# Who issues the loads: first-head loads moved to ScalarE, and the spare products spread out again

## The chip, the cores and the metric

One core of one Trainium2 chip. The metric is the device time of one execution in microseconds (us), lower is better. A run of the kernel is timed as a whole; the profile comes from one profiled execution, whose span runs from its first to its last instruction.

## The reference

The inputs are q, k, v and f_logit of shape (4, 8, 768, 48): batch, heads, tokens, head dimension. Weights are w_ch1 (384 x 1536) and w_ch2 (1536 x 384).

```python
f = 1 / (1 + exp(-f_logit))
for t in range(768):                       # per batch and head
    state = f[t, :, None] * state + outer(k[t], v[t])
    y[t] = q[t] @ state
x = y.transpose(0, 2, 1, 3).reshape(4, 768, 384)
u = x + real(fft(fft(x, axis=1), axis=2))
un = (u - mean(u)) / sqrt(var(u) + 1e-6)   # over the 384 channels
out = u + relu(un @ w_ch1) @ w_ch2
```

## The kernel before

Two heads make a **unit**; there are sixteen units, four to a batch. One head sits on partitions 0 to 47 of a tile and the other on 64 to 111 (`ROWS[0]`, `ROWS[1]`), tokens innermost. For every unit four things are read from memory: the gate logits `f` into `g`, then `k`, `q` and `v`. The `g`, `k` and `q` tiles come in two transfers of 144 KB each, one per head (r = 1 first, then r = 0), `v` in one of 288 KB. There are three buffers for `g` and `k` and four for `q`, used in turn, so a load of unit u overwrites what unit u - 3 (or u - 4) has used.

The generator `attention` works on one unit in steps, and each `yield` ends a step. By number: (1) ScalarE turns the logits into a log-gate with Exp and Ln (L330, L331); (2) VectorE scans it along the tokens (L337) and VectorE and GpSimd copy the ends of the chunks (L338, L339); (3) ScalarE takes three exponentials (L342, L343, L345); (4) VectorE multiplies q and k by two of them (L349, L350); (5) TensorE makes the scores (L361); (6) VectorE masks them (L368); (7) TensorE transposes, and ScalarE copies the result out (kT, L508); (8) to (12) are state, outputs and their transposes on TensorE, with copies by ScalarE (yT, L553 to L557, and x, L566); (13) `fold` combines tokens on VectorE and GpSimd.

After four units of a batch are done, `fnet` (letter F) computes the Fourier part (z, mid, mix), and `projected` (letter P) the two weight products: `up` at L750 with its relu on ScalarE at L752, and the second product at L759 or L773. H steps normalise.

The order of all this is written out by hand in one string, `ORDER`. Every engine's instructions are issued in the order of its words, and each engine works through its own list in order. A number advances that unit by one step. `L3fk` loads f and k of unit 3, `r` fetches one block of weights (`raw`) through SyncE, `R` three of them, `C` converts a block (ScalarE L238, VectorE L240 and L241, GpSimd L242), `T` loads the Fourier tables (`tab`, `wave`), `G` and `I` clear tiles, `W` combines weights, and `D` is `busy`: four spare bf16 products of 128 x 256 on TensorE (L153), whose result nobody reads.

All direct loads stand on SyncE's queue (SP), in ORDER's order: L166 for v, L170 for f, k and q, L267 for raw weights, L175 to L191 for the tables. If a transfer's buffer isn't free, SP waits and everything behind it on SP waits too. ScalarE (ACT) issues only one transfer, the last store (L624). The diff touches `load` and ORDER.

Of the kernel before, what the change touches and what calls it, by code (L numbers as in the profile page):

```python
# [12 lines left out]
C = 128  # L13
# [11 lines left out]


ORDER = (
    "Gq2 r I D Gq0 L0f Gk1 L1f D Gk0 L0q i D Gq3 C Gq1 Z L0k 0 D 1 Gk2 0 L1q 1 L1k D D D D D D D D D D D "
    "D 0 0 1 0 r 1 L2f 0 2 C L1v 1 L3fk 1 3 L0v 0 1 L2q 2 0 0 r 1 L2k 3 1 0 2 r 3 L3q 2 L2v 0 C L3v C "
    "L4fk R 4 2 2 3 1 0 C 2 4 1 3 L5qv D L4qv L5fk 3 D D 3 2 0 2 3 2 3 C r 4 1 4 L6fk C r 2 5 4 L6qv 4 2 "  # L30
    "1 5 6 3 4 D 4 C 5 3 T 3 6 4 5 5 4 2 r L7fk 7 5 D L7qv 3 5 S L8fk C 4 7 6 6 5 F0 5 r r F0 F0 F0 7 4 "
    "C F0 L9fk 5 6 8 H0 H0 6 5 6 r H0 C L8qv 6 7 L9qv P0 6 7 r C P0 7 7 C 9 P0 r r 5 8 C r C F0 r 7 F0 6 "
    "P0 5 9 C 6 7 P0 r C P0 8 8 C P0 r r 7 P0 P0 8 9 H0 C P0 P0 8 7 8 C P0 H0 7 9 6 H0 H0 C 9 r C P0 9 "
    "L10fk r 9 P0 r C 9 L11fk 10 C 6 P0 11 4 P0 P0 P0 P0 P0 P0 10 P0 P0 P0 L10qv P0 P0 7 F1 9 P0 F1 H0 9 "
    "W P0 P0 P0 11 F1 P0 L11qv P0 P0 P0 9 P0 P0 P0 8 L12fk P0 11 11 8 P0 P0 10 11 F1 P0 11 11 10 L14fk "
    "F1 8 P0 14 F1 P0 10 P0 8 10 P0 P0 H1 H1 10 L12qv P0 P0 10 P0 F1 P0 11 11 10 P0 10 H1 P0 P0 P0 P0 12 "
    "12 12 P0 P0 12 P0 H1 P0 12 P0 H1 L13fk P1 P1 P1 P1 P1 14 13 P1 12 8 8 P1 P1 12 9 10 L13qv 13 P1 P1 "
    "L14qv 9 P1 12 11 P1 H1 11 10 P1 P1 13 P1 13 P1 12 P1 P1 14 P1 14 V 13 P1 c V 10 P1 P1 P1 P1 P1 V "
    "L15fk P1 13 P1 11 V P1 P1 P1 P1 c P1 11 F2 V c F2 F2 H1 13 H1 F2 c 14 P1 c V c P1 P1 12 P1 P1 14 P1 "
    "P1 13 V V V P1 15 F2 c P1 12 P1 P1 P1 P1 c P1 H2 14 15 V V P1 P1 P1 P1 P1 13 P1 14 F2 P1 c P1 P1 15 "  # L40
    "V 13 P1 H2 P1 P1 L15qv P1 14 13 P1 V 12 H2 F2 14 P2 P2 P2 P2 P2 P2 P2 15 P2 P2 P2 c c 12 H2 V H2 15 "
    "H2 15 P2 c P2 15 P2 P2 15 P2 14 13 15 P2 P2 14 P2 P2 15 13 P2 P2 P2 P2 P2 H2 V 15 P2 P2 14 15 H2 P2 "
    "P2 P2 P2 15 F3 F3 P2 F3 F3 P2 F3 c P2 P2 P2 P2 P2 V P2 c P2 V c c V P2 P2 P2 P2 P2 c P2 F3 F3 P2 V "
    "P2 H3 P2 P2 P2 H3 H3 P2 P2 P2 P2 P2 P2 P2 P2 P2 P2 P3 H3 c P3 P3 P3 P3 V P3 c P3 P3 P3 c V V c P3 "
    "P3 P3 H3 P3 P3 P3 P3 P3 P3 c P3 P3 V P3 H3 P3 P3 P3 P3 P3 P3 H3 H3 P3 P3 P3 P3 P3 P3 P3 P3 P3 P3 P3 "
    "P3 V P3 P3 P3 P3 P3 c P3 c P3 P3 P3 M P3 P3 P3 P3 P3 P3 P3 P3 P3 P3 P3 P3"
)

PAIRS = ((0, 3), (2, 5), (1, 4))
# [4 lines left out]
def kernel(  # L54
# [13 lines left out]
    nc = tc.nc  # L68
    B, HP, _, D, _, S = qkf.shape
# [8 lines left out]
    R = 64 + D  # L78
    ROWS = [slice(64 * r, 64 * r + D) for r in range(2)]
# [79 lines left out]
    def load(u, *names):  # L159
        if u >= B * HP:  # L160
            return
        b, hp = divmod(u, HP)
        for name in names:
            if name == "v":
                v_of[u] = p3.tile([128, NCH, 2 * D], F32, tag="v", name=f"v{u}")
                nc.sync.dma_start(out=v_of[u], in_=v[b, hp])  # L166
                continue
            t, i = {"f": (g_t[u % 3], 2), "k": (k_t[u % 3], 1), "q": (q_t[u % 4], 0)}[name]
            for r in (1, 0):
                nc.sync.dma_start(out=t[ROWS[r]], in_=qkf[b, hp, r, :, i])  # L170

    def tables():

# [201 lines left out]
    def attention_by_blocks(u, x_all):  # L375
# [114 lines left out]
        T = double(64, T)  # L490
        yield
        load(u + 3, "f")
        yield from outputs(u, x_all, AT, Q, K, None, T)
        load(u + 3, "k")

    def outputs(u, x_all, AT, Q, K, te, T=None):
# [61 lines left out]
        if te is None:  # L558
            load(u + 4, "q", "v")
# [415 lines left out]
```

## Time and profile before

| | us |
|---|---|
| median of 3 runs (range) | 554.13 (553.52 to 554.17) |
| the profiled execution itself | 554.13 |
| its span | 552.4 |
| TensorE matmul busy (4186 instructions) | 528.4 |
| VectorE busy | 298.6 |
| ScalarE busy | 192.6 |
| GpSimd busy | 95.5 |

So 1.7 us of the execution lie outside the span. The mean granted TensorE clock is 0.981 of full speed. The page gives busy time by engine, busy shares in 40 equal slices of 13.8 us each, the DMA queues, the chain of work that ended last and the costliest groups. A group's busy time says how much work there is, not whether anybody waited for it; that is what the chain of waits and the timeline are for. Rows marked SPq or ACTq are transfers being issued by that engine's sequencer.

### The profile page before, as it was taken

What the parts mean: (1) busy time and instruction counts of PE and PEld (TensorE: products, weight loads), DVE (VectorE), ACT (ScalarE), POOL (GpSimd) and SP (SyncE); (2) the same over time, 40 slices, a digit from 0 to 9 for tenths busy, and PEclk for the clock granted to TensorE, in tenths of its full rate; (3) what the DMA queues carried; (4) which work ended last, traced back from release to release, by engine and by line L of the source; (5) the groups of instructions that cost most, each with busy time, mean ns of one, the idle gap of its engine ahead of it and who ended that gap; (6) DMA issues with size and microseconds to landing.
All of it is one profiled execution on the core that took longest, in us unless ns stands there. A gap on an engine that the chain in (4) does not pass through costs nothing.

```text
span 552.4 us, 10204 instructions
## 1 busy us (share of the span) xinstructions
PE 528.4 (96%) x4186; PEld 463.3 (84%) x4186; DVE 298.6 (54%) x534; ACT 192.6 (35%) x497; POOL 95.5 (17%) x147
## 2 busy tenths in 40 slices
PE   6888699999999999999999999999999999999995
PEld 5776578876898889889889899899889798989985
DVE  8999899984936427425644344444452442413231
ACT  5766476671332432541340422321411303021110
POOL 7156635434001000120101001003001000010000
PEclk9797799999999999999999999999999999999999
DMA  8989645363202100412530401002002004000001
GB/s 226 258 223 228 196 122 160 123 185 97 64 0 72 43 2 2 116 44 82 162 115 15 115 1 58 30 1 87 1 28 87 1 11 161 0 30 0 30 2 34
DMA packets 18398, 44.38 MB, mean 80 GB/s; under 512 B 3109, under 2 KB 4710, under 8 KB 18342
## 3 DMA queue, kind: packets, MB, share of 16 engines
q1 hardware_dynamic: 17094, 39.89, 25.8%
q0 software_dynamic: 1104, 3.54, 1.8%
q8 instruction: 35, 0.57, 0.4%
q10 hardware_dynamic: 144, 0.20, 0.1%
q14 instruction: 21, 0.17, 0.1%
HBM read 38.90 MB, written 4.72 MB: 79 GB/s over the span
## 4 chain that ended last, share of the span: by engine, by line
PE 87%; DMA 4%; DVE 3%; ACT 2%; SPq 1%; POOL 1%; issue 1%; ACTq 0%; POOLq 0%
PE up L750 34%; PE fx L773 16%; PE fz L773 12%; PE z L650 4%; PE y L537 3%; PE y L544 3%; PE po L759 3%; PE mix L669 3%; PE sc L361 3%; PE ds L517 2%; DMA g<-in_qkf_dram 2%; PE yt L564 2%; PE pt L708 1%; DMA raw<-in_w_ch_dram 1%; PE st L506 1%; DMA tab<-in_seq_tab_dram 1%
## 5 line engine op out<-in xcount | busy, mean ns | idle before, releaser
L750 PE MATMUL up<-unT,w 128*128 128x256 f32 x864 | 197.0, 382 | 1.5 <-DVE x L728 0.9
L750 PEld LDWEIGHTS up<-unT,w 128*128 128x128 f32 x864 | 161.0, 190 | 26.1 <-issue 1.5
L752 ACT ACTIVATE h<-up 128x256 f32<-128x256 f32 x144 | 55.2, 383 | 199.4 <-PE up L750 199.4
L617 POOL DMA_INDIRECT out_dram<-x,place x16 | 16.9, 1059 | 268.9 <-DVE x L803 232.0
L773 PE MATMUL fx<-block,h 128*128 128x192 f32 x264 | 46.5, 326 | 0.0
L773 PE MATMUL fx<-w,h 128*128 128x192 f32 x264 | 44.9, 327 | 0.1
L773 PEld LDWEIGHTS fx<-w,h 128*128 128x128 f32 x264 | 43.1, 190 | 0.8 <-ACT h L752 0.4
L773 PEld LDWEIGHTS fx<-block,h 128*128 128x128 f32 x264 | 43.5, 190 | 0.0
L242 POOL TENSOR_TENSOR w<-w,raw 128x384 uint32<-128x384 uint32 x24 | 30.3, 1267 | 47.6 <-ACT raw L238 19.1
L780 DVE TENSOR_TENSOR s<-h,h 128x768 f32<-128x768 f32 x11 | 10.5, 954 | 50.3 <-ACT h L752 50.3
L368 DVE COPY_PREDICATED at<-causal,sc 128x768 f32<-128x768 uint32 x32 | 31.2, 1030 | 0.8 <-PE sc L361 0.8
L337 DVE TENSOR_TENSOR_SCAN W<-g,bound 112x768 f32<-112x768 f32 x16 | 28.0, 1751 | 1.6 <-issue 0.9
L361 PE MATMUL sc<-q,W 48*64 48x128 f32 x768 | 24.9, 273 | 3.7 <-issue 1.4
L725 DVE TENSOR_TENSOR x<-mix,x 128x384 f32<-128x384 f32 x12 | 6.7, 556 | 39.0 <-PE mix L669 39.0
L361 PEld LDWEIGHTS sc<-q,W 48*64 48x64 f32 x768 | 20.9, 133 | 7.5 <-issue 3.6
L537 PE MATMUL y<-at,v 128*64 128x128 f32 (+1 forms) x384 | 26.9, 292 | 0.0
L537 PEld LDWEIGHTS y<-at,v 128*64 128x64 f32 (+1 forms) x384 | 23.2, 140 | 3.0 <-issue 3.0
L773 PE MATMUL fz<-w,s 128*128 128x192 f32 x132 | 23.5, 328 | 0.0
L773 PE MATMUL fz<-block,h 128*128 128x192 f32 x132 | 23.5, 328 | 0.0
L773 PE MATMUL fz<-w,h 128*128 128x192 f32 x132 | 23.4, 327 | 0.0
L544 PE MATMUL y<-q,stt 48*48 48x128 f32 x320 | 22.3, 285 | 0.0
L773 PEld LDWEIGHTS fz<-w,s 128*128 128x128 f32 x132 | 21.6, 190 | 0.3 <-issue 0.3
(145 smaller groups left out, 734.2 us busy)
## 6 DMA issues: line engine op xcount, KB each, us to landing
raw<-in_w_ch_dram SPq DMA_DIRECT2D x24, 384.0 KB, 4.4
g<-in_qkf_dram SPq DMA_DIRECT2D x32, 144.0 KB, 4.5
q<-in_qkf_dram SPq DMA_DIRECT2D x32, 144.0 KB, 4.0
k<-in_qkf_dram SPq DMA_DIRECT2D x32, 144.0 KB, 4.6
v<-in_v_dram SPq DMA_DIRECT2D x16, 288.0 KB, 5.2
k<-in_w_ch_dram SPq DMA_DIRECT2D x12, 384.0 KB
g<-in_w_ch_dram SPq DMA_DIRECT2D x12, 384.0 KB, 5.5
out_dram<-x SPq DMA_DIRECT2D x4, 168.0 KB
```

What stands on the lines that cost most here:

```text
L242: nc.gpsimd.tensor_tensor(bits, bits, lo, ALU.add)
L337: nc.vector.tensor_tensor_scan(W, g, bound[:R], 0.0, ALU.add, ALU.min)
L361: nc.tensor.matmul(ps[64 * s:64 * s + 64, r, i * C:(i + 1) * C], lhsT=W[ROWS[r], o + 64 * s:o + 64 * s + 64], rhs=Q[ROWS[r], o:o + C], sta ...
L368: nc.vector.copy_predicated(AT[:, :, half], causal.bitcast(U32).unsqueeze(1).unsqueeze(1).to_broadcast([128, 2, NCH // 2, C]), ps[:, :, :N ...
L537: nc.tensor.matmul(y[FILL[r], c * C:(c + 1) * C], lhsT=vt[:, c, r * D:r * D + (64 if r == 0 else D)], rhs=AT[:, r, c], start=(c % 4 == 0), ...
L544: nc.tensor.matmul(y[ROWS[r], c * C:(c + 1) * C], lhsT=st[ROWS[r], :, c - 1], rhs=Q[ROWS[r], c * C:(c + 1) * C], start=False, stop=True, s ...
L617: nc.gpsimd.indirect_dma_start(out=out.rearrange("b s d -> (b s) d"), out_offset=bass.IndirectOffsetOnAxis(ap=place[:, b, i:i + 1], axis=0 ...
L650: nc.tensor.matmul(z[:, cols], lhsT=src[:, j, lo:hi], rhs=tab[:, t, T % 2, cols], start=(i == 0), stop=(i == len(parts) - 1), skip_group_c ...
L669: nc.tensor.matmul(mix[:, o], lhsT=zz[:rows_of[T], T, PLACES[c]], rhs=cd[:rows_of[T], T, :NQ - odd], start=(i == 0), stop=(i == 1))
L750: nc.tensor.matmul(pp[:, :256], lhsT=w1[:, kt, m * 128:(m + 1) * 128], rhs=unT[:, kt], start=(kt == 0), stop=(kt == 2))
L752: nc.scalar.activation(hs[-1][:, m % H].rearrange("p t n -> p (t n)"), pp[:, :256], AF.Relu)
L773: nc.tensor.matmul(out, lhsT=h[:, m], rhs=blocks[i][:, m], start=(start and m == 0), stop=(m == H - 1), skip_group_check=True)
```

## The change

Two things. First, `load` issues the transfers of the first head (r = 0) of f, k and q through ScalarE; those of the second head (r = 1), and v, stay with SyncE. Second, the words `D` of ORDER are placed differently: the block of twelve after `L1k` shrinks to one, and thirteen are put elsewhere, mostly one by one. ORDER has 21 `D` before and 23 after. With all `D` left out, both ORDER strings are the same word by word.

```diff
-    "Gq2 r I D Gq0 L0f Gk1 L1f D Gk0 L0q i D Gq3 C Gq1 Z L0k 0 D 1 Gk2 0 L1q 1 L1k D D D D D D D D D D D "
-    "D 0 0 1 0 r 1 L2f 0 2 C L1v 1 L3fk 1 3 L0v 0 1 L2q 2 0 0 r 1 L2k 3 1 0 2 r 3 L3q 2 L2v 0 C L3v C "
-    "L4fk R 4 2 2 3 1 0 C 2 4 1 3 L5qv D L4qv L5fk 3 D D 3 2 0 2 3 2 3 C r 4 1 4 L6fk C r 2 5 4 L6qv 4 2 "
-    "1 5 6 3 4 D 4 C 5 3 T 3 6 4 5 5 4 2 r L7fk 7 5 D L7qv 3 5 S L8fk C 4 7 6 6 5 F0 5 r r F0 F0 F0 7 4 "
...
+    "Gq2 r I D Gq0 L0f Gk1 L1f D Gk0 L0q i D Gq3 C Gq1 Z L0k 0 D 1 Gk2 0 L1q 1 L1k D 0 0 1 0 r 1 L2f 0 2 "
+    "C L1v 1 L3fk D 1 3 L0v 0 1 L2q 2 0 0 r D 1 L2k 3 1 0 2 r 3 L3q 2 L2v D 0 C L3v D C L4fk R D 4 2 2 3 "
+    "1 0 C 2 4 1 3 L5qv D L4qv L5fk 3 D D 3 2 0 2 3 2 3 C r 4 1 4 L6fk C r 2 5 4 D L6qv 4 D 2 1 5 6 3 4 "
+    "D 4 C 5 3 D T 3 6 4 5 5 4 2 r L7fk 7 5 D L7qv 3 5 S L8fk C 4 7 6 6 5 F0 5 r r F0 F0 F0 7 4 C F0 "
+    "L9fk 5 6 8 H0 H0 6 5 6 r D D H0 D C L8qv 6 7 L9qv P0 6 7 r C P0 7 7 C 9 P0 r r 5 8 C r C F0 r 7 F0 "
+    "6 P0 5 9 C 6 7 P0 r C P0 8 8 C P0 r r 7 P0 P0 8 9 H0 C P0 P0 8 7 8 C P0 H0 7 D 9 6 H0 H0 C 9 r C P0 "
...
+    "9 W P0 D P0 P0 11 F1 P0 L11qv P0 P0 P0 9 P0 P0 P0 8 L12fk P0 11 11 8 P0 P0 10 11 F1 P0 11 11 10 "
...
             for r in (1, 0):
-                nc.sync.dma_start(out=t[ROWS[r]], in_=qkf[b, hp, r, :, i])
+                queue = nc.scalar if r == 0 else nc.sync
+                queue.dma_start(out=t[ROWS[r]], in_=qkf[b, hp, r, :, i])
```

## The prediction, made before the changed kernel was run

> **What bounds the kernel now.** I read the page's slices first, then busy time by stages of 10 us, the chain of waits, SP's waits and ScalarE's timeline up to 70 us.
>
> ```profile
> PE   6888699999999999999999999999999999999995
> PEclk9797799999999999999999999999999999999999
> DMA  8989645363202100412530401002002004000001
> ```
>
> TensorE is full from the sixth slice on. In the first five, 69 us, it isn't, its granted clock drops, and the DMA engines are at eight or nine tenths. So time can be won or lost in two ways: by what delays the start, and by what adds TensorE work later. The busy-time windows confirm it (columns: window and length, busy us of PE, PEld, DVE, ACT and POOL with instruction counts, PE clock, DMA share, GB/s).
>
> ```profile
> 10.00:20.00 10.00, 7.40 (x132) 6.06 (x131) 9.89 (x13) 7.92 (x13) 2.68 (x9) 0.95 1.04 249
> 20.00:30.00 10.00, 9.55 (x151) 8.68 (x151) 9.13 (x14) 7.43 (x15) 1.08 (x3) 0.71 1.04 261
> 70.00:80.00 10.00, 10.00 (x116) 8.05 (x114) 9.40 (x17) 7.18 (x24) 4.29 (x3) 0.99 0.37 100
> 90.00:100.00 10.00, 10.00 (x101) 8.45 (x100) 9.62 (x19) 6.96 (x18) 5.90 (x6) 1.00 0.46 149
> ```
>
> From 10 to 30 us the DMA engines are saturated at about 250 GB/s. From 70 us TensorE has no idle time to give back, so a delay at 70 us stays to the end. The timeline shows how closely SP runs ahead of ScalarE:
>
> ```profile
> 8.64 0.89 SPq L170 DMA_DIRECT2D g<-in_qkf_dram  x2
> 12.88 0.78 SPq L170 DMA_DIRECT2D g<-in_qkf_dram  x2
> 14.57 0.48 ACT L345 ACTIVATE te<-deep,low 112x240 f32<-112x240 f32 x1
> 14.96 0.83 ACT L330 ACTIVATE g<-g 112x768 f32<-112x768 f32 x1
> 17.21 0.83 ACT L330 ACTIVATE g<-g 112x768 f32<-112x768 f32 x1
> 20.60 0.63 ACT L508 COPY kT<-st 128x560 f32<-128x560 f32 x1 [1.60 <-PE st L506]
> 23.15 0.89 SPq L170 DMA_DIRECT2D g<-in_qkf_dram  x2
> 30.45 0.84 ACT L330 ACTIVATE g<-g 112x768 f32<-112x768 f32 x1 [0.69 <-DMA g<-in_qkf_dram]
> 57.19 0.64 ACT L566 COPY x<-yt 128x576 f32<-128x576 f32 x1 [0.89 <-PE yt L564]
> 64.48 0.84 ACT L330 ACTIVATE g<-g 112x768 f32<-112x768 f32 x1 [6.65 <-DMA g<-in_qkf_dram]
> ```
>
> SP issues f of unit 2 at 8.64, of unit 3 at 12.88, of unit 4 at 23.15. ScalarE uses them at 14.96, 17.21 and 30.45: leads of 6.3, 4.3 and 7.3 us. SP can do this because it isn't held by ScalarE's computing.
>
> [...] the DMA share is 1.04 with one issuer, and one load costs SP about 0.43 us. [...] no row of this trace shows a transfer issued by ScalarE between two ACTIVATEs[...]. [...] mean clock 0.71 from 20 to 30 us, and 24 products y take 2.82 us at 48.16 against 1.52 at 29.48.
>
> **Part one, the loads.** All 48 r = 0 transfers of f, k and q leave SP and stand in ScalarE's list where ORDER has them: 48 x 0.43 = 20.6 us of issuing. The only ACTq issue of the trace takes 0.38, so ScalarE pays 18 to 21 us of sequencer time, most beside idle ACT (192.6 busy of 552.4). The price that matters is lead. For landing I use 5.5 us: the issue table gives medians of 4.0 to 4.6, but for 0 to 35 us, under saturation, 4.7 to 5.7.
>
> *Unit 2.* ORDER has `1 L2f 0 2`: the load now stands behind unit 1's exponentials. Their last releaser (the copy of `deep` on GpSimd) is done at 12.0, so a sequencer that runs ahead issues at about 12.3 and the logits land at 17.8. Exp of unit 2 moves from 14.96 to 17.8.
>
> *Unit 3.* `2 C L1v 1 L3fk D 1 3`: the sequencer was held at Exp of unit 2 until 17.8, issues then (17.9), and the landing is at 23.4, against 17.21 now. ScalarE is in order, so kT of unit 0, behind it, starts after Exp and Ln (0.95 + 0.84) at 25.2 instead of 20.60: **+4.6**. The products ds and y of unit 0 wait for that, and with them the start.
>
> *Unit 4.* `0 C L3v D C L4fk R D 4`: the load stands behind the yT copies, which wait for y at 27.6 + 4.6 = 32.2. Issued at 32.3, landed at 37.8; without a new stall Exp would be at 30.45 + 4.6 = 35.05: **+2.8**, together +7.4.
>
> *Units 5, 6, 8 and 9* have their load two or more ScalarE groups ahead of Exp (unit 6: about 42.5 for 48.80), so I put nothing; the cover is ScalarE's copies, and if it went they would cost up to 2 us each.
>
> *Unit 7.* `L7fk 7`: again no distance. But ScalarE already stands here for 6.65 us waiting for this tile, with 10 us from issue to landing behind the tables on SP. Now r = 0 is issued at the x copy, 57.19 + 7.4 + 0.1 = 64.7, and lands at 70.2, against 64.48: **+5.7** remains of +7.4. The SP half should be no later, since SP has issued nine loads fewer by then.
>
> *After 70 us* ScalarE's relus stand behind the moved loads: 0.4 to 0.8 us each time. L10f and L11f come late for their Exp by 1 to 2 us, but ScalarE's next relu after those is only at 137.25, 10.7 us after. I put +0.3 in all; 0 to 3 are the ends.
>
> **Part two, the spare products.** One D costs 0.49 us (12 instructions at 34.81 took 1.47). Eleven leave the block, which fills TensorE from 3.94 to 13.45 and ends before the first scores at 13.78. Nothing waits for it[...]. If the first 48 scores run at half speed, 1.54 becomes 1.54 x 2.82 / 1.52 = 2.86, +1.3 on a chain whose kT is already 4.6 late through ScalarE: hidden, and back if that stall doesn't come. Eight are added between 14 and 50 us, where TensorE has 15 us idle up to 70: nothing by my choice, from -3 (a half-clock stretch avoided) to +4 (each in the way). Five are added after 78 us: `r D D H0 D C`, `7 D 9`, `W P0 D P0`. There TensorE is full: 5 x 0.49 = 2.45, less the 0.67 us idle from 80 to 85 us: **+1.8**.
>
> Sum: 5.7 + 0.3 + 1.8 = +7.8, rounded down a little for the SP issue time saved, one issue of 0.43: **+7.4**, on 554.13 (the profiled execution's time, which is also the median): **561.5 us**.
>
> **Rivals.** (1) *ScalarE's sequencer doesn't run ahead*, or waits for counters shared with SP's transfers (SP itself waited 4.8 us at q of unit 7 for `wave`, a tile it doesn't touch). Then unit 2's load is issued when te ends at 15.05, landing 20.55; Exp, Ln and C (2.35) follow, unit 3's load goes at 22.9, lands at 28.4, kT at 30.2: +9.6. Unit 4: copies and C end at 29.76 + 9.6 = 39.36, landing 44.9 against 40.05: +14.4. Unit 7: 57.83 + 14.4 + 5.5 = 77.7, +13.2. With 1.8 and 0.3: 569.4 us. For it: nothing in the trace shows running ahead past a transfer. [...]
>
> (2) *SP's relief wins* (the other side). The chain of waits runs through SP and DMA from 33.6 to 64.5:
>
> ```profile
> 34.44 1.33 SPq L166
> 39.14 7.49 DMA raw<-in_w_ch_dram
> 47.03 6.28 DMA tab<-in_seq_tab_dram
> 53.32 0.94 SPq L170
> 54.31 10.09 DMA g<-in_qkf_dram
> ```
>
> If ScalarE's loads don't queue behind raw and tab, g of unit 7 can land in 5.5 instead of 10.09 (-4.6), and four r = 0 issues leave that chain (-1.7). With +1.8 for D: 549.6 us. It decides only if kT of unit 0 stays at 20.60, so only if unit 3's load isn't late. Against it: the DMA engines are saturated whoever issues, and both halves of a tile are needed.
>
> (3) *The transfers are the limit anyway*, and unit 7's wait swallows all of the delay: +1.8 for D and little else, 556 us, or, if the spread D save a half-clock stretch, no change.
>
> That the change doesn't do what it says I exclude: both edits are in the diff, and nothing but D differs in ORDER.
>
> **How the numbers follow.** Forecast 57%, rival 1 26%, rival 2 7%, rival 3 10% (about half of it within 0.2%). 0.2%, 1.1 us, is about what a measurement of this kernel can tell from no change. Faster 0.07 (rival 2 and a piece of 3, less what the stalls of 2 keep), same 0.05, slower 0.88. The range 555.5 to 572 leaves out rival 2, the no-change part of 3, and rival 1 with three or more half-clock microseconds on top.
>
> **What would show it.** Right: Exp of units 2, 3 and 4 wait for DMA g on ScalarE, 2 to 6 us each; kT of unit 0 starts near 25; after 70 us TensorE is as full as now, with L153 rows among `up`. Wrong: ACTq L170 rows well before the ACTIVATEs that ORDER has ahead of them, kT of unit 0 near 20.6, or a lasting loss spread over the relus after 140 us rather than at the start.

## The result, and the profile after

The changed kernel takes 569.65 us (568.05 to 570.89, 4 runs) against 554.15 for the kernel before on the same chip: 1.0277 times as long, 95% interval 1.0247 to 1.0308. That is 15.5 us more where +7.4 was forecast: the direction is right, the size is twice what I put. The profiled execution has a span of 568.4 us.

The page's slices of the changed kernel, 14.2 us each:

```profile
PE   3588769999999999999999999999999999999995
PEclk9998879999999999999999999999999999999999
DMA  8947845525301210140641300201002005000001
```

TensorE is still full from the seventh slice on. The loss is ahead of that. The third DMA digit, for 28 to 43 us, is 4 where 8 stood before, so the transfers are no longer the limit there. Busy time by stages (window and length, busy us of PE, PEld, DVE, ACT, POOL with counts, PE clock, DMA share, GB/s):

```profile
10.00:20.00 10.00, 5.90 (x98) 5.11 (x99) 9.05 (x12) 5.72 (x10) 1.43 (x8) 1.00 1.05 238
20.00:30.00 10.00, 2.79 (x18) 2.33 (x18) 2.80 (x3) 3.02 (x6) 1.20 (x2) 1.00 0.88 218
70.00:80.00 10.00, 5.76 (x101) 4.75 (x96) 7.00 (x15) 2.35 (x5) 5.24 (x16) 0.84 0.56 150
90.00:100.00 10.00, 9.13 (x144) 7.60 (x142) 8.64 (x17) 7.88 (x21) 1.10 (x2) 1.00 0.61 160
```

From 20 to 30 us every compute engine now stands for 7 us or more: TensorE 2.79 busy instead of 9.55, ScalarE 3.02 instead of 7.43. A second hole is at 70 to 80 us. The timeline says what ScalarE waits for (start, us, engine, operation; in brackets the idle time before and what ended it; ACTq is a transfer being issued):

```profile
13.65 0.32 ACTq L171 DMA_DIRECT2D g<-in_qkf_dram  x1
18.14 0.84 ACT L331 ACTIVATE g<-g 112x768 f32<-112x768 f32 x1 [3.32 <-DMA g<-in_qkf_dram]
19.11 0.84 ACT L332 ACTIVATE g<-g 112x768 f32<-112x768 f32 x1
19.17 0.32 ACTq L171 DMA_DIRECT2D g<-in_qkf_dram  x1
27.44 0.84 ACT L331 ACTIVATE g<-g 112x768 f32<-112x768 f32 x1 [6.95 <-DMA g<-in_qkf_dram]
29.15 1.13 ACT L509 COPY kT<-st 128x560 f32<-128x560 f32 x2
36.71 0.32 ACTq L171 DMA_DIRECT2D g<-in_qkf_dram  x1
39.79 0.84 ACT L331 ACTIVATE g<-g 112x768 f32<-112x768 f32 x1 [0.99 <-DMA g<-in_qkf_dram]
71.97 0.32 ACTq L171 DMA_DIRECT2D g<-in_qkf_dram  x1
78.08 0.84 ACT L331 ACTIVATE g<-g 112x768 f32<-112x768 f32 x1 [7.62 <-DMA g<-in_qkf_dram]
```

These are four pairs of issue and wait, for f of units 2, 3, 4 and 7. The lead is gone: each load is issued when ScalarE gets to it, and ScalarE then stands until it lands, 18.9 us in four waits. The chain of waits has two of these landings in it, 4.47 and 8.25 us, where before it had none ahead of 39 us:

```profile
13.65 4.47 DMA g<-in_qkf_dram
18.14 0.94 ACT g L331 x2
19.17 8.25 DMA g<-in_qkf_dram
27.44 0.94 ACT g L331 x2
```

Where the time went, as the start of the same ScalarE instruction against the kernel before, in us. "kT" is the copy for unit 0, "Exp 4" and "Exp 7" the first exponential of units 4 and 7, then the first and the last relu (before: 20.60, 30.45, 64.48, 86.19 and 532.50). The last column is the median against the runs of before on the same chip. A row of offsets comes from one profiled execution, which lies up to 3 us from its median.

| run | kT | Exp 4 | Exp 7 | first relu | last relu | median |
|---|---|---|---|---|---|---|
| changed kernel | +8.6 | +9.3 | +13.6 | +15.3 | +15.9 | +15.5 |
| loads only | +7.4 | +7.2 | +13.8 | +13.4 | +13.2 | +15.3 |
| spare products only | +0.1 | +0.3 | +0.8 | +1.3 | +1.9 | +4.4 |
| units 2 and 3 on SP | +2.1 | +5.2 | +7.7 | +9.4 | +10.0 | +10.1 |
| only units 2 and 3 on ScalarE | +8.4 | +9.3 | +11.8 | +13.1 | +13.7 | +12.9 |
| units 8 to 15 on ScalarE | +0.5 | +0.5 | -1.2 | +4.3 | +5.0 | +5.0 |
| k and q only | +0.1 | +1.6 | +5.8 | +6.0 | +6.7 | +6.2 |
| k and q only, block of before | +0.2 | +0.8 | -0.9 | +1.9 | +1.8 | +3.8 |
| f only, block of before | +6.8 | +6.3 | +9.6 | +9.9 | +9.9 | +12.0 |

From the first relu on, at 86 us before, every row is flat to within 0.8 us. So in the profiled executions nearly all of the loss is in the start.

### The profile page after: what moved, and what is told of

Same layout as the page of the kernel before. It is cut to its first block, busy times and chain, and to the rows that moved or that the text cites. A ratio compares the mean times of both kernels' runs of the same rounds, so it can differ in the third digit from the quotient of the medians.

```text
span 568.4 us, 10216 instructions
## 1 busy us (share of the span) xinstructions
PE 530.7 (93%) x4194; PEld 465.3 (82%) x4194; DVE 300.0 (53%) x534; ACT 192.5 (34%) x497; POOL 94.2 (17%) x147
## 4 chain that ended last, share of the span: by engine, by line
PE 84%; DVE 6%; DMA 3%; ACT 3%; POOL 2%; issue 1%; ACTq 0%; SPq 0%; POOLq 0%; DVEq 0%
PE up L751 33%; PE fx L774 15%; PE fz L774 12%; PE z L651 4%; PE y L538 3%; PE po L760 3%; PE sc L362 3%; PE mix L670 3%; PE y L545 2%; PE ds L518 2%; DMA g<-in_qkf_dram 2%; DVE at L369 1%; PE yt L565 1%; PE pt L709 1%; PE y L153 1%
## 5 line engine op out<-in xcount | busy, mean ns | idle before, releaser
L243 POOL TENSOR_TENSOR w<-w,raw 128x384 uint32<-128x384 uint32 x24 | 28.7, 1201 | 56.9 <-ACT raw L239 34.1
L781 DVE TENSOR_TENSOR s<-h,h 128x768 f32<-128x768 f32 x11 | 10.5, 955 | 50.1 <-ACT h L753 50.1
L362 PE MATMUL sc<-q,W 48*64 48x128 f32 x768 | 27.9, 295 | 5.8 <-DVE W L351 5.2
L362 PEld LDWEIGHTS sc<-q,W 48*64 48x64 f32 x768 | 23.8, 146 | 9.8 <-DVE W L351 5.6
L518 PE MATMUL ds<-v,kT 128*64 128x48 f32 (+3 forms) x320 | 15.8, 248 | 12.0 <-ACT kT L509 10.8
L518 PEld LDWEIGHTS ds<-v,kT 128*64 128x64 f32 (+1 forms) x320 | 12.5, 149 | 16.6 <-ACT kT L509 11.6
L538 PE MATMUL y<-at,v 128*64 128x128 f32 (+1 forms) x384 | 25.7, 283 | 0.0
L153 PE MATMUL y<-bound 128*128 128x256 bf16 x92 | 15.7, 323 | 8.9 <-ACT yT L558 5.0
```

The costliest lines, as they stand in the source:

```text
L153: nc.tensor.matmul(spare, lhsT=bound[:, :C], rhs=bound[:, :2 * C], start=not started, stop=True, skip_group_check=True)
L243: nc.gpsimd.tensor_tensor(bits, bits, lo, ALU.add)
L362: nc.tensor.matmul(ps[64 * s:64 * s + 64, r, i * C:(i + 1) * C], lhsT=W[ROWS[r], o + 64 * s:o + 64 * s + 64], rhs=Q[ROWS[r], o:o + C], sta ...
L518: nc.tensor.matmul(ds[FILL[r], :, c:c + n], lhsT=kT[:, c, FILL[r]], rhs=vt[:, c, r * D:(r + 1) * D].unsqueeze(2).to_broadcast([128, D, n]) ...
L538: nc.tensor.matmul(y[FILL[r], c * C:(c + 1) * C], lhsT=vt[:, c, r * D:r * D + (64 if r == 0 else D)], rhs=AT[:, r, c], start=(c % 4 == 0), ...
```

## The experiments

**The two parts apart.** First, the order of before with the new `load`; second, the new order with the old `load`.

```diff
 ORDER = (order of before)
-                nc.sync.dma_start(out=t[ROWS[r]], in_=qkf[b, hp, r, :, i])
+                queue = nc.scalar if r == 0 else nc.sync
+                queue.dma_start(out=t[ROWS[r]], in_=qkf[b, hp, r, :, i])
```

> The loads part alone: the order of before with its block of twelve spare products, first-head loads on ScalarE. Late-load theory: nearly the whole loss, +13 to +15 us over before (567 to 569), kT of unit 0 near 28 to 29 us. Rival, spare products carry a large part: at most +8 (562). Rival, issue time and relus behind it: the same total, but kT of unit 0 stays under 25 us and the loss grows after 100 us.

569.38 us, ratio 1.0277 (1.0245 to 1.0309): the whole loss, and kT at 28.05.

```diff
-ORDER = (order of before)
+ORDER = (order after; load as before)
```

> The spare products alone placed as in the changed kernel, all loads on SyncE. Late-load theory: +1 to +3 us over before (555 to 557), from five D in the full stage (2.45 us) and cold first scores (+1.3). Rival, spare products carry a large part: +6 or more (560).

558.52 us, ratio 1.0072 (1.0052 to 1.0093). That is +4.4 us, more than the +1 to +3 expected and less than the rival's +6. Beside the loads the spare products add nothing that can be told (569.65 and 569.38), so there their cost must lie under the same waits. The runs spread from 555.8 to 559.6, and the profiled one, at 555.89, is among the fastest: its offset of +1.9 is all that a trace locates.

**Which units.** `and u not in (2, 3)`, then `and u in (2, 3)`, then `and u >= 8` added to the condition of the new `load`.

> The changed kernel, but both heads of units 2 and 3 loaded by SyncE. Late-load theory: Exp of unit 3 returns to 17 to 19 us, kT of unit 0 to 21 to 22, and 7 to 9 us of the 15.5 come back (560 to 563); what is left is units 4 and 7 and the spare products. Rival, issue time and relus: only 4 of 48 issues are taken out, 569 stays within 1.5 us.

564.19 us, ratio 1.0173 (1.0135 to 1.0211). Exp of unit 3 starts at 19.35 and kT at 22.74. 5.5 us come back, fewer than expected, because Exp of unit 4 now waits by itself: its offset goes from +2.1 at kT to +5.2.

> Only the first-head loads of units 2 and 3 on ScalarE, all others on SyncE, spare products as in the changed kernel. Late-load theory: kT of unit 0 near 28 to 29 us, +8 to +11 us over before (562 to 565). Rival, issue time and relus: as the spare products alone, 555 to 557.

567.04 us, ratio 1.022 (1.0187 to 1.0252), kT at 29.04. With the spare products in both runs, two units cost 12.9 us, more than the 8 to 11 expected, and the other fourteen 10.1. The units do not add: a wait that is taken away leaves the next one to show.

> First-head loads on ScalarE for units 8 to 15 only (24 of 48), spare products as in the changed kernel. Lead theory: every point up to the first up product as with the spare products alone, total within 1 us of that run (557.5 to 559.5). Rival, issue time on ScalarE holds the relus up after 70 us: 2 us or more above it, growing between the tenth relu and the last.

558.93 us, ratio 1.0079 (1.0057 to 1.0101), against 1.0072 for the spare products alone. Half of all the transfers stand on ScalarE and cost nothing that can be told. The rival that ScalarE's issue time holds up the relus falls.

**Lead, with ScalarE still the issuer.** Words are moved forward in the new order; who issues is unchanged.

```diff
-L1k D 0 0 1 0 r 1 L2f 0 2 C L1v 1 L3fk D 1 3
+L1k L2f D 0 0 1 0 r 1 L3fk 0 2 C L1v 1 D 1 3
```

> The changed kernel with the words L2f and L3fk put earlier (L2f right after L1k, L3fk ahead of the first step of unit 2), so that ScalarE issues them some 4 us sooner; who issues what is unchanged. Lead theory: Exp of unit 3 at 19 to 21 us instead of 27.4, kT of unit 0 at 21 to 23 instead of 29.15, and the total near that of SyncE loading units 2 and 3 (562 to 565). Rival, ScalarE is simply a worse issuer (issue time, its own queue served later): kT of unit 0 stays at 27 or later, total within 2 us of 569.7.

566.52 us, ratio 1.0215 (1.0179 to 1.0251). The start of that run's timeline:

```profile
9.32 0.43 ACTq L171 DMA_DIRECT2D g<-in_qkf_dram  x1
13.53 0.32 ACTq L171 DMA_DIRECT2D g<-in_qkf_dram  x1
15.55 0.84 ACT L331 ACTIVATE g<-g 112x768 f32<-112x768 f32 x1 [0.90 <-DMA g<-in_qkf_dram]
17.80 0.84 ACT L331 ACTIVATE g<-g 112x768 f32<-112x768 f32 x1
21.55 0.62 ACT L509 COPY kT<-st 128x560 f32<-128x560 f32 x1 [1.95 <-PE st L507]
```

Issued 4.3 and 5.6 us sooner, f of units 2 and 3 is in time, Exp of unit 3 is at 17.80 instead of 27.44, and kT is 0.95 us late instead of 8.55. For this stretch it matters when the load is issued; that ScalarE issues it costs little. But the loss only falls from 15.5 to 11.6 us, where 562 to 565 was expected for the total: the delay comes back later, +2.8 at Exp of unit 4, +10.5 at Exp of unit 7.

```diff
-0 1 L2q 2 0 0 r D 1 L2k 3 1 0 2
+0 1 L2q L2k 2 0 0 r D 1 3 L4fk 1 0 2
...
-5 3 D T 3 6 4 5 5 4 2 r L7fk 7
+5 3 D L7fk T 3 6 4 5 5 4 2 r 7
```

> As the one before, with L4fk, L2k and L7fk put earlier too; all 48 first-head loads still on ScalarE. Lead theory: Exp of unit 4 and of unit 7 no longer wait 3.5 us each, total 556 to 560, that is little more than the spare products alone cost. Rival, ScalarE is a worse issuer: 565 or more.

569.37 us, ratio 1.0271 (1.0219 to 1.0322): a miss. kT is at 22.73, but the x copy of unit 3 comes at 72.93, 15.7 us late, and the total is no better than the changed kernel's. The next run names the reason. For that, the same with `L2q L2k` put before the first step of unit 2 and `L4fk` and `L3q` earlier still:

```diff
-L3fk 0 2 C L1v 1 D 1 3 L0v 0 1 L2q L2k 2 0 0 r D 1 3 L4fk 1 0 2 r 3 L3q 2 L2v
+L3fk L2q L2k 0 2 C L1v 1 D 1 3 L4fk L0v 0 1 L3q 2 0 0 r D 1 3 1 0 2 r 3 2 L2v
```

> All 48 first-head loads on ScalarE, as in the changed kernel, with L2f, L3fk, L2q, L2k, L4fk, L3q and L7fk all put earlier in the order. If lead alone is the price: kT of unit 0 and of unit 2 both within 3 us of before, total 557 to 561. If ScalarE's loads also hold SyncE up through the eight completion counters that both share: kT of unit 0 is near before, but later points still slip by 5 us or more and the total stays at 563 or more.

567.09 us, ratio 1.0212 (1.0175 to 1.0249). The second expectation held, and the timeline names the place:

```profile
62.61 0.32 ACTq L171 DMA_DIRECT2D g<-in_qkf_dram  x1
72.48 0.32 ACTq L171 DMA_DIRECT2D k<-in_qkf_dram  x1
72.84 0.64 ACT L567 COPY x<-yt 128x576 f32<-128x576 f32 x1 [11.12 <-DMA wave<-in_dim_tab_dram]
```

ScalarE does nothing for 11.12 us ahead of a copy whose input doesn't come from `wave`. In the order, the load of k of unit 7 stands just ahead of that copy. In the trace each transfer counts its landing on one of eight semaphores, which SP's and ScalarE's transfers use in turn (135 and 49 of them in the changed kernel), and a transfer waits until the one before it on its semaphore has landed (the changed kernel's trace has all sixteen parts of the one before ahead of 165 of 176 such issues); for this k the one before is a `wave` transfer of SP, issued at 60.50, whose last part landed at 72.46. ScalarE, in order, holds its copies meanwhile. In the kernel before the same kind of wait (4.8 us for `wave`) stood on SP, where no computing is queued behind it.

Unit 7 is not the only place. In the loads-only run a copy kT stands behind a load of k that waits for a q transfer of SP; TensorE had the copy's input ready at 45.6, so some 3.5 of the 7.12 us are the counter's:

```profile
48.74 0.32 ACTq L171 DMA_DIRECT2D k<-in_qkf_dram  x1
49.10 0.63 ACT L509 COPY kT<-st 128x560 f32<-128x560 f32 x1 [7.12 <-DMA q<-in_qkf_dram]
```

To test the hold at unit 7, that unit is taken off ScalarE in the kernel with the loads put earlier:

```diff
-                queue = nc.scalar if r == 0 else nc.sync
+                queue = nc.scalar if r == 0 and u != 7 else nc.sync
```

> As the run with L2f, L3fk, L2q, L2k, L4fk, L3q and L7fk put earlier (567.1), but both halves of unit 7 are loaded by SyncE. Counter theory: ScalarE's 11 us stand before the x copy of unit 3 goes, that copy is within 8 us of before instead of 15.7, and the total falls by 5 to 9 us, to 558 to 562. Rival, the stand only shifts to the tables or to TensorE: 565 or more.

566.19 us, ratio 1.0201 (1.0164 to 1.0239). The 11 us are gone: the copy is at 63.73, +6.5 instead of +15.7, and Exp of unit 7 at 64.27, 0.2 earlier than before. The total hardly moves: kT of unit 5 then waits for TensorE until 72.83, and the first relu is 12.4 us late. The rival was right about the total. With the block of twelve spare products of before instead of the spread ones, `L7fk` at its place of before, and all else as there:

```diff
-L1k L2f D 0 0 1 0 r 1 L3fk L2q L2k 0 2 C L1v 1 D 1 3
+L1k L2f D D D D D D D D D D D D 0 0 1 0 r 1 L3fk L2q L2k 0 2 C L1v 1 1 3
```

> First-head loads on ScalarE except for unit 7, loads put earlier as in the run before, and the spare products as in the kernel before (block of twelve). If late f loads, the counter hold at unit 7 and the spare products are all there is: 554 to 558. Rival, sharing the eight counters slows SyncE in every stretch up to 70 us: 559 or more.

559.48 us, ratio 1.0112 (1.0073 to 1.0151). 45 of the 48 first-head loads still stand on ScalarE here, and most of the loss is gone. But 5.7 us are left in the median (+5.1 at the first relu), and the total is on the rival's side of my line. The profile has them before unit 7 (kT +2.9, x copy of unit 1 +6.8), and shows the counters at work on ScalarE again:

```profile
18.20 0.32 ACTq L171 DMA_DIRECT2D k<-in_qkf_dram  x1
18.62 0.84 ACT L331 ACTIVATE g<-g 112x768 f32<-112x768 f32 x1 [3.74 <-DMA k<-in_qkf_dram]
23.11 0.32 ACTq L171 DMA_DIRECT2D k<-in_qkf_dram  x1
23.47 1.15 ACT L509 COPY kT<-st 128x560 f32<-128x560 f32 x2 [0.79 <-DMA g<-in_qkf_dram]
```

Each of the two loads of k is issued when a transfer of SP on its semaphore has landed (at 18.18 and 23.04), and Exp of unit 2 and kT of unit 0 come right behind. From the run before to this one the first relu came 7.3 us forward (+12.4 to +5.1), with the spare products and the place of `L7fk` changed together: with the loads early, the spread products seem no longer to be free.

**What lies ahead of a load.** Two raw fetches of 384 KB, which SP issues ahead of the load of unit 3 in time, though they stand behind it in the order, are moved to behind the load of unit 4.

```diff
-0 0 r D 1 L2k 3 1 0 2 r 3 L3q 2 L2v D 0 C L3v D C L4fk R D 4
+0 0 D 1 L2k 3 1 0 2 3 L3q 2 L2v D 0 L3v D L4fk r r D 4 C C R
```

> The changed kernel with two raw fetches of 384 KB (and the conversions that need them) moved from before the load of unit 3 to after it, so that SyncE has 768 KB less under way when ScalarE issues that load at 19.2 us. If ScalarE's load is served only after what SyncE issued earlier: landing takes 5 to 5.5 us instead of 8.25 (768 KB at 240 GB/s are 3.2 us), Exp of unit 3 at 24 to 24.7 us, kT of unit 0 near 26. If the engines take turns between the two queues: landing stays 7 to 8.5 us. The total tells less, since raw comes later.

573.6 us, ratio 1.0347 (1.0307 to 1.0387), 4 us more than the changed kernel. The load of unit 3 was issued later, at 20.95, so Exp of unit 3 is no earlier (27.37), and landed after 6.4 us, between the two expectations:

```profile
20.95 0.32 ACTq L171 DMA_DIRECT2D g<-in_qkf_dram  x1
27.37 0.84 ACT L331 ACTIVATE g<-g 112x768 f32<-112x768 f32 x1 [5.10 <-DMA g<-in_qkf_dram]
```

The landing time alone doesn't settle how the two queues share the engines. The DMA view tells more. In the changed kernel, first the stretch 19.5 to 22.5 us, just after that load was issued at 19.17, then 22.5 to 25.5 (queue q1 is SP's, q10 ScalarE's; packets, MB, share of 16 engines):

```profile
q1 hardware_dynamic: 318, 0.79, 103.0%
```

```profile
q1 hardware_dynamic: 216, 0.45, 66.9%
q10 hardware_dynamic: 120, 0.28, 36.8%
```

For three microseconds the engines move 0.79 MB for SP, and not one packet of ScalarE's. SP had issued two v, two k, two q halves and two raw blocks between 13.5 and 19 us, and ScalarE's load was served behind them. From its issue to the first packet on q10 3.8 us passed, in which SP's queue moved 1.00 MB; in the run with less ahead it was 2.6 us and 0.53 MB. With nothing of SP's under way (the q issued at 34.93 in the changed kernel) it was 0.96 us. So in these three cases ScalarE's load began the later, the more SP had under way. It is not the whole of the 8.25 us: the trace has this landing in sixteen parts, fifteen of them were there at 25.40, and the last came at 27.41.

**Which tensors.** `and name != "f"` in the new kernel; then the same with the order of before; then `and name == "f"` with the order of before.

> Only k and q of the first heads on ScalarE, both halves of f on SyncE, spare products as in the changed kernel. If the loads of f, which ScalarE itself waits for, carry the loss: Exp of units 2, 3, 4 and 7 within 2 us of before and the total 558 to 562. Rival, any transfer on ScalarE costs alike: two thirds of the loss stay (565 or so).

560.16 us, ratio 1.009 (1.0058 to 1.0122). kT is at 20.74. With the 16 transfers of f back on SP, 9.5 of the 15.5 us are gone, though 32 transfers stay on ScalarE. Exp of unit 7 is still 5.8 us late, where I expected at most 2.

> Only k and q of the first heads on ScalarE, f on SyncE, spare products as in the kernel before. With the spread spare products this cost 560.2, the spread alone 558.5. If the two add: 555.5 to 557. Rival, the spare products only hid under the same waits: 559 or more.

557.59 us, ratio 1.0063 (1.0047 to 1.0079): k and q by themselves cost 3.8 us in the median, a little more than expected. The profiled execution, one of the faster (556.31), locates 1.8 of them.

> Only f of the first heads (16 transfers) on ScalarE, k and q on SyncE, spare products as in the kernel before. If late f loads carry the loss by themselves: kT of unit 0 at 26 to 29 us, total 563 to 568. If it takes k and q as well: kT of unit 0 under 25, total under 561.

565.9 us, ratio 1.0224 (1.0203 to 1.0245), kT at 27.41: f alone costs 12 us. The two costs, 12.0 and 3.8, add up to the 15.3 of all the loads or a little more. Unit 7 in its trace:

```profile
62.30 0.32 SPq L171 DMA_DIRECT2D g<-in_qkf_dram  x1
63.36 0.32 ACTq L171 DMA_DIRECT2D g<-in_qkf_dram  x1
74.09 0.84 ACT L331 ACTIVATE g<-g 112x768 f32<-112x768 f32 x1 [10.10 <-DMA g<-in_qkf_dram]
```

ScalarE's half, issued as soon as ScalarE comes to it, lands after 7.0 us, at 70.4. The wait goes on until SP's half, issued 1.06 us earlier, has landed at 74.07, after 11.8 us. Fifteen of that half's sixteen parts were there at 66.63; only the last was missing. It was so in the kernel before, too (58.07 and 64.40 for the half that ended the wait of 6.65 us). In both traces a `wave` transfer of 97 rows that SP issued shortly ahead has its last part 11.6 and 9.8 us after its issue (60.42 in the kernel before), and SP's next transfers get their last part after it (the next raw block, g and k there at 63.69 to 65.01). Whether this transfer holds up one part of those that follow is not shown: no run changes it.

**Is there something to gain?** Three kernels with all loads on SP and the spare products of before.

```diff
-L6qv 4 2 1 5 6 3 4 D 4 C 5 3 T 3 6 4 5 5 4 2 r L7fk 7      (before)
+L6qv 4 2 1 5 6 3 4 D 4 C 5 3 L7fk T 3 6 4 5 5 4 2 r 7      (first)
+L6qv T 4 2 1 5 6 3 4 D 4 C L7fk 5 3 3 6 4 5 5 4 2 r 7      (second)
+L6qv L7fk T 4 2 1 5 6 3 4 D 4 C 5 3 3 6 4 5 5 4 2 r 7      (third)
```

First, only `L7fk` ahead of `T`:

> The kernel before, all loads on SyncE, with only L7fk put ahead of T, so that f and k of unit 7 don't stand behind the tables. If the 6.65 us wait of ScalarE for f of unit 7 sets the start: 1 to 4 us faster (550 to 553). Rival, the tables set it as well: no change within 1 us.

554.81 us, ratio 0.9993 (0.9978 to 1.0009): no change, though Exp of unit 7 starts at 57.01, 7.5 us earlier. kT of unit 5, next to it, is only 1.7 us earlier, and the first relu not at all. Second, `T` right after `L6qv` and `L7fk` after them:

> The kernel before, all loads on SyncE, with the tables T asked for right after L6qv and L7fk after them but ahead of unit 5's exponentials. Putting L7fk ahead alone moved Exp of unit 7 by 7.5 us and the total by nothing, because the tables and TensorE were no earlier. If the tables are what is late next: 1 to 3 us faster (551 to 553.5). Otherwise no change, or slower where unit 5 and 6 lose their place behind the tables.

553.49 us, ratio 0.9986 (0.9975 to 0.9997). Third, `L7fk` and then `T` right after `L6qv`:

> The kernel before, all loads on SyncE, with L7fk and then T asked for right after L6qv. Having the tables earlier gave 0.5 us, having f of unit 7 earlier gave nothing by itself. If both were late for each other: 1 to 3 us faster than before (551 to 553). Otherwise within 1 us of it.

554.38 us, ratio 1.001 (0.9999 to 1.002). The second is the only version with a median below that of the kernel before beyond its interval, by 0.14%: less than the 0.2% that I can tell with confidence, so no more than a hint. The 6.65 us wait at unit 7, the longest on ScalarE's list before, was worth nothing.

## Why the prediction was right in kind and wrong in size

**The mechanism and its place: right.** The loads of units 2, 3, 4 and 7 come late on ScalarE, kT of unit 0 goes with them, nothing is lost after 70 us for ScalarE's issue time, and the spare products hide behind the waits. The f-only run and the units-8-on run show both sides of this.

**Where the sum went wrong,** in the profiled execution: kT of unit 0 came out 4.0 us later than I put, the step from there to Exp of unit 4 cost 2.0 less, the step from Exp of unit 4 to Exp of unit 7 cost 6.0 more (+4.3 instead of -1.7), and the rest about 0.6 more. That makes 8.5 us, from +7.4 to +15.9.

**Unit 2: right, by two errors.** Exp at 18.14 against 17.8. The issue came at 13.65 instead of 12.3 (that the sequencer runs ahead there was my estimate; no row of the trace before showed it), the landing took 4.47 instead of 5.5.

**Unit 3: the term that was mis-sized.** "The sequencer was held at Exp of unit 2 until 17.8, issues then (17.9), and the landing is at 23.4." Measured: issue 19.17, landing 27.44. Of the 4.0 us too few, 0.3 came from unit 2, 1.0 from the issue and 2.75 from the landing. The issue: Ln waited for Exp's result (there at 19.07) through ScalarE's own semaphore, and the sequencer with it: the load behind Ln was issued at 19.17, after Ln had started at 19.11. The landing: 8.25 us where I put 5.5, a figure for all of 0 to 35 us. At this place SP had 1.00 MB ahead, and for the SP load of q issued at 19.3 the trace before had 6.9. Much of the price was there to be read at the right place. kT became +8.55 instead of +4.6.

**Unit 4: too dear.** I put +2.8. The offset rose from 8.55 to 9.34: with SP held up, the DMA share from 30 to 40 us is 0.25, and the load landed in 3.1 us.

**Unit 7: the step that failed.** I let the wait of before swallow part of the delay, +7.4 to +5.7; it rose from +9.3 to +13.6. The load should have been issued at 64.7 and have landed at 70.2; Exp came at 78.08, 7.9 us later. First, ScalarE reached the x copy of unit 3 at 69.82 and not at 64.6. Of these 5.2 us 1.9 were there at Exp of unit 4 already, and 3.3 came up in between, at units 5 and 6, where I had put nothing. Second, the load was not issued 0.1 us after the start of that copy but 2.15 us after it, at 71.97, when a `wave` transfer on whose semaphore it waits had landed (71.95). I had named such waits, but only in rival 1. Third, it didn't land in 5.5 us but in 6.1. Taking a load off the busy queue didn't take it off the busy engines: their share was 0.71 from 71.97 to 78.08, 0.45 of it SP's. That the SP half would be no later held here, but not in the f-only run.

**k and q: a term left out.** I priced only f. Alone k and q cost 3.8 us, and in the run with f of units 2 and 3 early VectorE stood 2.85 us for q of unit 2, which ScalarE had issued at 22.04 and which landed at 29.52. They are also what came up between Exp of unit 4 and the x copy of unit 3: with f alone on ScalarE the offset stays there (+6.3 and +6.2), with all the loads and the same block of spare products it goes from +7.2 to +13.9, and the hold of 3.5 us behind a load of k, shown above, is part of that.

**The spare products: right in the full stage, low in the start.** The two D after the first relu cost 0.8 us together (offset 15.32 to 16.13), where 2 x 0.49 is 1.0; alone, the spread cost 4.4 in the median against +1.8. One cause is in the trace of the changed kernel:

```profile
37.78 1.03 PE L153 MATMUL y<-bound 128*128 128x256 bf16 x8 [1.14 <-ACT yT L558]
38.74 1.52 PE L362 MATMUL sc<-q,W 48*64 48x128 f32 x45
```

A spare product writes into the tile that also holds y, and waits until the yT copies have read it. Here it stands ahead of scores whose inputs were ready at 36.3, and holds TensorE for its own time and for that wait. Such waits are 5.0 us, in four, in the changed kernel and 3.8, in three, with the spare products alone; before there are none. I had costed D at its own time only.

The forecast for the first scores came true: with the block gone TensorE is idle for 5.16 us ahead of the first scores, and 48 of them take 2.84 us (forecast 2.86) instead of 1.54. Half speed was my estimate, from the 2.82 and 1.52 us of the products y. The clock column's 1.00 from 10 to 20 us doesn't show it; the products' own durations do. But I said that this would come back if ScalarE's stall didn't, and with the loads on SP kT is only 0.1 us late. The mean clock of 0.71 from 20 to 30 us in the kernel before (0.50 from 20 to 24) has no such idle time ahead of it: from 3.94 us on to 19 us, where that slow stretch begins, TensorE had not been idle for more than 1.4 us at a time. What began it is not shown.

**Rival 1** gave 569.4 with 26%, and the total lies there. Of its two mechanisms the first, a sequencer that doesn't run ahead at all, is not what happened (13.65 lies ahead of the te exponential at 14.34); the second, counters shared with SP, is, at unit 7 and, in other runs, before it. Its stations were +9.6, +14.4 and +13.2; measured were +8.6, +9.3 and +13.6. So part of the agreement is luck.

What stays open: in the run with loads early, unit 7 on SP and the old block, 5.7 us remain. Its trace has holds by the shared semaphores in that stretch, but no run takes the semaphores apart, so how much of the 5.7 us they are is not shown. Nor is it shown what makes up the spare products' 4.4 us, of which the profiled execution has only 1.9.

## What to carry to other kernels

Count the lead of each load, from issue to first use, at its own place, and compare it with the landing time read at that same place; a load moved to an engine that computes in order keeps only the lead that its place in that engine's program gives (f of unit 3: 4.3 us of lead before, a wait of 6.95 us after). A second queue brought no bandwidth to engines that were saturated (238 GB/s from 10 to 20 us, 249 before), and it made ScalarE stand for a landing counter (11.12 us ahead of one copy), a wait that held up no computing on SP (4.8 us before). If some loads must go there, choose those with long leads: the 24 of the late units cost nothing that can be told (558.93 us against 558.52), the 16 of f cost 12 us.

## What the runs showed of the hardware that I had not expected

- Two queues on the same engines did not take turns here. A load on ScalarE's queue, issued at 19.17 us, got no packet from 19.5 to 22.5 us while SP's earlier transfers moved 0.79 MB: at its start it behaved as one line in order of issue. It isn't always so: in the f-only run ScalarE's half of unit 7 landed 3.7 us ahead of the SP half that was issued before it. When the one holds and when the other is not shown.
- ScalarE's sequencer ran ahead, but little: in the changed kernel a load was issued 0.06 us after the start of the ACTIVATE ahead of the last one (13.59 and 13.65), or 0.06 us after the start of one that waits for its own engine's result (19.11 and 19.17). The second load did not get past that wait.
- A transfer's landing hung on one of its sixteen parts: 6.3 of the 10.09 us of unit 7's f in the kernel before passed between the fifteenth and the last.
- Of ScalarE's 49 issues in the changed kernel 46 take 0.32 to 0.45 us of its sequencer, and the other three up to 1.5. The median is 0.32 us, and 0.36 for SP's.
